# Logits of a soft mixture of experts: four 128-row pieces of g at a time in every second step, in place of two in every step

## The chip, the cores and the metric

The kernel runs on one core of one Trainium2 chip. The metric is the device time of one execution in microseconds, and the time of a kernel is the median of several runs. The engines are called by their names: TensorE (PE in the profile, PEld for its weight loads), VectorE (DVE), ScalarE (ACT), GpSimd (POOL) and SyncE (SP, which only issues DMAs here).

## What is computed

Three stages in float32: attention by chunks of 32 positions with a small context, a feed-forward layer with a rational activation, and a soft mixture of experts.

```python
x = chunk_attention(q, k, v, mem_k, mem_v)     # 3072 tokens x 512
h = x @ w_in                                   # 3072 x 2048
P = a[0] + a[1]*h + a[2]*h**2 + a[3]*h**3
Q = 1.0 + abs(b[0])*abs(h) + abs(b[1])*h**2
g = P / (Q + 1e-6)
x = g @ w_out                                  # 3072 x 512
logits = x @ phi                               # 3072 x 32 slots
d = softmax(logits, axis=0); slot_input = d.T @ x      # 8 experts x 4 slots
slot_out[e] = relu(slot_input[e] @ w1[e]) @ w2[e]      # per expert
out = softmax(logits, axis=1) @ slot_out
```

The kernel never forms `g @ w_out` for all tokens. It uses `wp = w_out @ phi` (2048 x 32), so that logits = g @ wp, and keeps a running sum of d.T @ g, to which w_out is applied once at the end.

## The kernel before

The tokens go in six blocks of 512 (numbered 0 to 5), and the 2048 columns of h in 8 steps of 256 per block. So there are 48 steps k; i = k % 8 is the step's place in its block. One iteration kk of the outer loop (line 569) holds work of several steps, listed in `KN` (line 24) and carried out by `run_step`:

- `h0`, `h1`: the two halves (128 columns each) of h for step kk + 1, 12 float32r matmuls of 128x512 each (`h_part`, line 309). They read x, split in two parts (tiles `xt`), and write one of two PSUM tiles `h`.
- `a1`, `d1`, `a2`, `t`: the rational function of step kk on ScalarE (lines 527, 528, 530, 546, 547) and VectorE (529, 540, 541), a refinement of the reciprocal on POOL (504), and, one iteration later, its end on VectorE (555, 556), which leaves g in a tile `T` (five tiles rotate).
- `p0`, `p1`: `post(k, part)` for step k = kk - 2 (`LATER`: nothing at i = 2, and the steps kk - 3 and kk - 2 at i = 3). Part 0 first does the logits of the step (line 326): two 128x32 pieces of wp as stationary operand against the two 128x512 pieces of g, each piece writing its own strip of 32 rows of one PSUM bank `lg`. The four strips j = 0 to 3 belong to four consecutive pieces of g, so an even step (o = 0) writes strips 0 and 1 and an odd one (o = 1) strips 2 and 3. The strips are summed over the block, and `soft1` adds the four together. Each part then transposes four 128x128 pieces of g into a PSUM bank (line 334), and ScalarE copies them to a tile `g` (line 335). Steps come in pairs that share a `g` tile (`qd`).
- `x1`, `x2`, `x3`: the softmax pieces of the block before. `soft1` (line 341, at i = 1) copies the logits, sums the strips with a matmul (345) and does the running maximum and exponentials (351 to 363); `soft2` (at i = 2) transposes the weights to tokens (370); `soft3` (at i = 2) adds d.T @ g with 16 matmuls of four 32-column pieces each (387), which are four strips side by side as well.
- `at`: one slice of the attention of the block to come (the generator `attention`, line 144). A block has two pairs of 128-token tiles, 18 slices a pair: two of q-k scores (161), six of softmax on VectorE and ScalarE (179 to 188), two of transposes of the weights (196, 198), two of products with v (206), two of normalisation (216), and four of transposes into x and its split (225, 229, 230). Loads of q and k are issued in a pair's third slice, of v in its twelfth. `h0` at i = 7 carries out all slices that are left, for step kk + 1 then belongs to the next block.

Block 0 has a list of its own (`ord0`, with conversions of the weights mixed in), blocks 1 to 4 use `ord`, and the last block, which has no attention to prepare, uses `ordl`. After step 47 iterations 48 and 49 finish the last two steps; the expert part follows, whose weights are loaded into tiles as they come free (`fill`).

The lists give priority. The framework that builds the program keeps data dependences, waits for free tiles, and may put an instruction ahead of one listed earlier that isn't ready yet; so the order of an engine in the trace isn't always the order of the code.

In the profile one float32 matmul of line 326, 345 or 387 is two MATMUL instructions (two passes), one of line 309 or a transpose is one.

Of the kernel before, what the change touches and what calls it, by code (L numbers as in the profile page):

```python
# [19 lines left out]
def float_of_bits(u):  # L20
# [3 lines left out]
KN = {  # L24
    'pre': "q0 i0 v0 q1 o0 v1 i1 o1 s0 A A A A A A A A A A n0 B B B B B B B B B B A A A A A A B B w0 B B B B i2 s1 o2 n1 z0 q2 v2 i3".split(),
    'ord0': "at a1 w1 s2 h0 d1 at t o3 z1 i4 n2 at a2 h1 p0 at p1 at at".split(),
    'ord': "at a1 h0 d1 at t a2 x2 at h1 p0 x1 at p1 x3 at".split(),
    'ordl': "a1 h0 d1 t a2 x2 h1 p0 x1 p1 x3".split(),
}


# [10 lines left out]
def tile_chunk_attention__rational__soft_moe(  # L42
# [15 lines left out]
    PE, ACT, DVE, POOL, SP = nc.tensor, nc.scalar, nc.vector, nc.gpsimd, nc.sync  # L58
# [15 lines left out]
    NF = DFF // P  # L74
# [29 lines left out]
    def bank(shape):  # L104
        return ps_m("m", shape)
# [7 lines left out]
    wp = const("wp", [P, NF, NSLOT])  # L113
# [142 lines left out]
    a0, a1, a2, a3 = (ctab[:, n:n + 1] for n in range(4))  # L256
# [57 lines left out]
    st = {}  # L314

    def post(k, part):

        b, i = divmod(k, NSTEP)
        qd, o = divmod(i, 2)
        t_ = gt_tile[k]  # L320
        if part == 0:
            if i == 0:
                st["lg"] = ps_l("lg", [P, BLK])
            for f2 in range(2):
                j = 2 * o + f2
                PE.matmul(st["lg"][32 * j:32 * j + 32, :], lhsT=wp[:, 2 * i + f2, :], rhs=t_[:, f2, :],  # L326
                          start=(qd == 0), stop=(qd == NF // 4 - 1))
            if o == 0:
                gts[b, qd] = p_g("g", [P, TT, 4 * P])
        pb = bank([P, 2, 2 * P])  # L330
        for m in range(2):
            for f2 in range(2):
                tt = 2 * part + m
                PE.transpose(pb[:, m, f2 * P:f2 * P + P], t_[:, f2, tt * P:tt * P + P], ident)  # L334
        ACT.activation(gts[b, qd][:, 2 * part:2 * part + 2, 2 * P * o:2 * P * o + 2 * P], pb, AF.Copy)  # L335
        if part:
            del gt_tile[k]

    m_run, den, neg_m, alpha = (run[:, n:n + 1] for n in range(4))

# [112 lines left out]
    hs, gt_tile = {}, {}  # L453
# [36 lines left out]
    def w_out_rows(ft):  # L490
        return got["o", ft // 2][:, ft % 2, :]
# [77 lines left out]
    for kk in range(total + 4):  # L569
        b, i = divmod(kk, NSTEP)  # L570
# [31 lines left out]
    for n in range(4):  # L602
        for j in range(4):
            ft = 4 * j + n
            PE.matmul(pb[32 * j:32 * j + 32, :], lhsT=ut[:, n, 32 * j:32 * j + 32],
                      rhs=w_out_rows(ft),
                      start=(n == 0), stop=(n == 3))
# [11 lines left out]
    for eq in range(2):  # L619
        hb = ps_h("h", [P, 2, 512])  # L620
        for c in range(NC):
            for hh in range(2):
                for j in range(4):
                    e = 4 * eq + j
                    PE.matmul(hb[32 * j:32 * j + 32, hh, :], lhsT=sz[:, c, e, :],  # L625
                              rhs=got[("1", e, c)][:, 512 * hh:512 * hh + 512], start=(c == 0), stop=(c == NC - 1))
# [5 lines left out]
        h1 = p_a4("a4", [P, 2, 512])  # L632
# [16 lines left out]
    for eq in range(2):  # L649
        for n in range(8):  # L650
            for j in range(4):
                PE.matmul(so[32 * j:32 * j + 32, :], lhsT=hts[eq][:, n, 32 * j:32 * j + 32],
                          rhs=got[("2", 4 * eq + j, n // 2)][:, n % 2, :],
                          start=(eq == 0 and n == 0), stop=(eq == 1 and n == 7))
# [82 lines left out]
```

## Time and profile before

| | |
|---|---|
| time, median of 3 runs | 634.65 us (632.43 to 635.01) |
| the profiled execution | 633.84 us, span 632.1 us |
| TensorE busy | 561.1 us (89%), weight loads 377.0 us (60%) |
| VectorE busy | 461.8 us (73%) |
| ScalarE busy | 421.4 us (67%) |
| GpSimd busy | 123.5 us (20%) |
| line 309 (h), TensorE | 291.1 us, 1152 instructions |
| line 326 (logits), TensorE | 54.0 us, 192 instructions |
| line 334 (transposes of g), TensorE | 58.2 us, 384 instructions |
| line 387 (soft3), TensorE | 23.5 us, 192 instructions |
| mean granted clock of TensorE | 0.971 of full speed |

The span runs from the first to the last instruction of the profiled execution; the time of that execution includes what lies around it. Busy time of a group is the union of its instructions, so instructions side by side count once; the mean duration of one is another matter, since matmuls are pipelined. The span has four parts: about 64 us of loads and conversions until the first step's activation starts, block 0 with conversions of weights (to 153 us), blocks 1 to 5 (to about 533 us), and a tail with the last softmax, the experts and the output.

### The profile page before, as it was taken

To read this page: it belongs to the slowest core of one execution; us is meant where nothing else is said; L and a number is where in the kernel's file an instruction comes from. 1 tells how busy PE (TensorE), PEld (TensorE's weight loads), DVE (VectorE), ACT (ScalarE), POOL (GpSimd) and SP (SyncE) were. 2 spreads that over 40 slices of the span, in tenths; PEclk is the share of its full clock that TensorE was granted. 3 is DMA by queue.
4 is the path that set the end of the run, shared out by engine and by line. 5 is a ranking of instruction groups with operands and counts; after the bars stand their busy time and mean duration, and the time that the engine had idled before them with its cause. 6 is when DMAs were issued, how large, how long until landed. Compare 5 with 4: busy or idle time off the path is not lost.

```text
span 632.1 us, 13355 instructions
## 1 busy us (share of the span) xinstructions
PE 561.1 (89%) x5784; PEld 377.0 (60%) x5784; DVE 461.8 (73%) x578; ACT 421.4 (67%) x542; POOL 123.5 (20%) x74
## 2 busy tenths in 40 slices
PE   1349999999999999999999999999999997489965
PEld 1338886767666776667765667656776574235211
DVE  3775799977997869978699786997877957620022
ACT  2576899988775878758777586776869688310022
POOL 0121122321231312313133131322223322000000
PEclk9999999999999999999999999999999999689985
DMA  7996745320212202121022210321175236779936
GB/s 308 414 369 218 314 150 200 108 94 1 102 69 90 78 2 101 68 102 67 3 100 68 99 50 21 101 68 63 53 270 184 70 131 226 298 282 409 405 143 266
DMA packets 21754, 97.39 MB, mean 154 GB/s; under 512 B 3136, under 2 KB 3136, under 8 KB 16704
## 3 DMA queue, kind: packets, MB, share of 16 engines
q1 hardware_dynamic: 18000, 79.70, 33.6%
q0 software_dynamic: 2880, 16.78, 7.2%
q8 instruction: 45, 0.74, 0.5%
q10 hardware_dynamic: 816, 0.07, 0.1%
q14 instruction: 13, 0.11, 0.1%
HBM read 86.05 MB, written 10.49 MB: 153 GB/s over the span
## 4 chain that ended last, share of the span: by engine, by line
PE 56%; DVE 18%; ACT 12%; issue 6%; DMA 6%; POOL 1%; DVEq 0%; POOLq 0%; ACTq 0%; SPq 0%
PE h L309 28%; PE lg L326 6%; PE m L334 5%; PE m L387 4%; DMA g<-in_moe_w_in_dram 3%; DVE T L540 3%; DVE T L541 2%; DVE T L555 2%; PE h L625 2%; ACT S L528 2%; ACT g L335 2%; DVE S L529 2%; ACT T L530 2%; DVE T L556 2%; PE h L668 2%
## 5 line engine op out<-in xcount | busy, mean ns | idle before, releaser
L309 PE MATMUL h<-xt,win 128*128 128x512 f32 x1152 | 291.1, 401 | 1.2 <-DVE T L541 0.8
L309 PEld LDWEIGHTS h<-xt,win 128*128 128x128 f32 x1152 | 209.6, 189 | 46.7 <-DVE T L541 1.3
L504 POOL TENSOR_TENSOR S<-S,S 128x1024 f32<-128x1024 f32 x46 | 110.7, 2407 | 315.8 <-DVE S L529 291.0
L529 DVE SCALAR_TENSOR_TENSOR S<-S,S 128x1024 f32<-128x1024 f32 (+1 forms) x49 | 58.8, 1200 | 51.3 <-ACT S L528 51.3
L527 ACT ACTIVATE S<-h,ctab 128x1024 f32<-128x1024 f32 (+1 forms) x49 | 53.7, 1097 | 58.0 <-PE h L309 56.1
L334 PEld LDWEIGHTS m<-ident,T 128*128 128x128 f32 x384 | 42.1, 143 | 46.2 <-issue 22.6
L335 ACT ACTIVATE g<-m 128x512 f32<-128x512 f32 x96 | 55.6, 603 | 18.1 <-PE m L334 18.1
L540 DVE TENSOR_TENSOR T<-T,h 128x1024 f32<-128x1024 f32 (+1 forms) x49 | 58.2, 1188 | 7.6 <-ACT T L530 7.6
L541 DVE SCALAR_TENSOR_TENSOR T<-T,ctab,h 128x1024 f32<-128x1024 f32 (+1 forms) x49 | 61.5, 1254 | 1.3 <-DVE T L540 0.4
L326 PE MATMUL lg<-T,wp 128*32 128x512 f32 x192 | 54.0, 620 | 9.0 <-DVE T L556 9.0
L555 DVE SCALAR_TENSOR_TENSOR T<-T,ctab,S 128x1024 f32<-128x1024 f32 (+1 forms) x49 | 61.3, 1252 | 0.1
L334 PE MATMUL m<-ident,T 128*128 128x128 f32 x384 | 58.2, 285 | 2.3 <-DVE a L182 1.2
L556 DVE SCALAR_TENSOR_TENSOR T<-S,T 128x1024 f32<-128x1024 f32 (+1 forms) x49 | 58.7, 1199 | 1.8
L530 ACT ACTIVATE T<-h,ctab 128x1024 f32<-128x1024 f32 (+1 forms) x49 | 58.9, 1201 | 0.0
L547 ACT ACTIVATE S<-S,ctab 128x1024 f32<-128x1024 f32 (+1 forms) x49 | 55.9, 1144 | 0.6
L546 ACT ACTIVATE S<-S 128x1024 f32<-128x1024 f32 (+1 forms) x49 | 51.5, 1053 | 5.8 <-DVE S L529 3.2
L528 ACT ACTIVATE S<-h,ctab 128x1024 f32<-128x1024 f32 (+1 forms) x49 | 53.7, 1095 | 0.9 <-DVE T L555 0.9
L675 DVE TENSOR_SCALAR xt<-h,csum 128x512 f32<-128x512 f32 x12 | 8.5, 746 | 30.8 <-PE h L668 30.8
L387 PE MATMUL m<-g,ptok 128*32 128x512 f32 x192 | 23.5, 634 | 0.4 <-ACT ptok L372 0.4
L183 ACT ACTIVATE a<-a 128x512 f32<-128x512 f32 x22 | 14.0, 638 | 14.1 <-DVE a L182 14.1
L230 DVE TENSOR_TENSOR xt<-m,xt 128x512 fp32r<-128x512 f32 x24 | 16.5, 688 | 8.5 <-ACT xt L229 8.5
L268 ACT ACTIVATE g<-g 128x1024 uint32<-128x1024 uint32 x16 | 18.5, 1156 | 5.3 <-DMA g<-in_moe_w_in_dram 4.1
(155 smaller groups left out, 614.3 us busy)
## 6 DMA issues: line engine op xcount, KB each, us to landing
win<-in_moe_w_dram SPq DMA_DIRECT2D x32, 512.0 KB, 5.1
k<-in_kw_dram SPq DMA_DIRECT2D x11, 1024.0 KB, 7.4
v<-in_vw_dram SPq DMA_DIRECT2D x11, 1024.0 KB, 4.8
g<-in_moe_w_in_dram POOLq DMA_DIRECT2D x6, 1024.0 KB, 7.3
g<-in_moe_w_out_dram POOLq DMA_DIRECT2D x6, 1024.0 KB, 9.1
out_dram<-xt SPq DMA_DIRECT2D x12, 512.0 KB, 3.2
q<-in_qw_dram SPq DMA_DIRECT2D x11, 512.0 KB, 3.8
T<-in_moe_w_dram SPq DMA_DIRECT2D x10, 512.0 KB, 10.0
```

The lines of the kernel that those rows point to most:

```text
L309: PE.matmul(tile_[:, f2, :], lhsT=ww[:, c, f2 * P:f2 * P + P], rhs=xx[:, c, :], start=(n == 0), stop=(n == 3 * NC - 1))
L326: PE.matmul(st["lg"][32 * j:32 * j + 32, :], lhsT=wp[:, 2 * i + f2, :], rhs=t_[:, f2, :], start=(qd == 0), stop=(qd == NF // 4 - 1))
L334: PE.transpose(pb[:, m, f2 * P:f2 * P + P], t_[:, f2, tt * P:tt * P + P], ident)
L335: ACT.activation(gts[b, qd][:, 2 * part:2 * part + 2, 2 * P * o:2 * P * o + 2 * P], pb, AF.Copy)
L504: (POOL if k < total - 2 else DVE).tensor_tensor(out[:, o], q[:, o], w[:, o], ALU.mult)
L528: ACT.activation(y[:, o], hh[:, o], AF.Square, scale=rb1)
L529: DVE.scalar_tensor_tensor(s[:, o], y[:, o], QC, s[:, o], ALU.add, ALU.add)
L530: ACT.activation(t[:, o], hh[:, o], AF.Identity, bias=a2, scale=a3)
L540: DVE.tensor_tensor(t[:, o], t[:, o], hh[:, o], ALU.mult)
L541: behind[kk] = DVE.scalar_tensor_tensor(t[:, o], t[:, o], a1, hh[:, o], ALU.add, ALU.mult).ins
L555: DVE.scalar_tensor_tensor(t[:, o], t[:, o], a0, w[:, o], ALU.add, ALU.mult)
L556: DVE.scalar_tensor_tensor(t[:, o], e[:, o], 2.0, t[:, o], ALU.subtract, ALU.mult, reverse0=True)
```

## The change

The even step of a pair no longer does its two logits matmuls. The odd step does all four: pieces 0 and 1 from the T tile of the step before, pieces 2 and 3 from its own, in one group of four matmuls, each with its strip of 32 rows. So there are 24 groups of four matmuls where there were 48 of two, with the same 96 matmuls in all. The T tile of an even step is read until then, and both references are dropped after the odd step's second part.

In the lists `ord` and `ordl` the order changes as well. In `ord` the third attention slice, which stood between x2 and h1, and the fourth, which stood behind x1 ahead of p1, are both listed behind p1 and x1 now, one on either side of x3; `soft1` (x1) is listed behind both parts of `post` where it stood between them. `ordl` has this last move alone. `ord0` and `LATER` stay.

```diff
--- before.py
+++ after.py
@@ -24,8 +24,8 @@
 KN = {
     'pre': "q0 i0 v0 q1 o0 v1 i1 o1 s0 A A A A A A A A A A n0 B B B B B B B B B B A A A A A A B B w0 B B B B i2 s1 o2 n1 z0 q2 v2 i3".split(),
     'ord0': "at a1 w1 s2 h0 d1 at t o3 z1 i4 n2 at a2 h1 p0 at p1 at at".split(),
-    'ord': "at a1 h0 d1 at t a2 x2 at h1 p0 x1 at p1 x3 at".split(),
-    'ordl': "a1 h0 d1 t a2 x2 h1 p0 x1 p1 x3".split(),
+    'ord': "at a1 h0 d1 at t a2 x2 h1 p0 p1 x1 at x3 at at".split(),
+    'ordl': "a1 h0 d1 t a2 x2 h1 p0 p1 x1 x3".split(),
 }
 
 
@@ -321,20 +321,21 @@
         if part == 0:
             if i == 0:
                 st["lg"] = ps_l("lg", [P, BLK])
-            for f2 in range(2):
-                j = 2 * o + f2
-                PE.matmul(st["lg"][32 * j:32 * j + 32, :], lhsT=wp[:, 2 * i + f2, :], rhs=t_[:, f2, :],
-                          start=(qd == 0), stop=(qd == NF // 4 - 1))
             if o == 0:
                 gts[b, qd] = p_g("g", [P, TT, 4 * P])
+            else:
+                for j in range(4):
+                    PE.matmul(st["lg"][32 * j:32 * j + 32, :], lhsT=wp[:, 4 * qd + j, :],
+                              rhs=gt_tile[k - 1 + j // 2][:, j % 2, :],
+                              start=(qd == 0), stop=(qd == NF // 4 - 1))
         pb = bank([P, 2, 2 * P])
         for m in range(2):
             for f2 in range(2):
                 tt = 2 * part + m
                 PE.transpose(pb[:, m, f2 * P:f2 * P + P], t_[:, f2, tt * P:tt * P + P], ident)
         ACT.activation(gts[b, qd][:, 2 * part:2 * part + 2, 2 * P * o:2 * P * o + 2 * P], pb, AF.Copy)
-        if part:
-            del gt_tile[k]
+        if part and o:
+            del gt_tile[k - 1], gt_tile[k]
 
     m_run, den, neg_m, alpha = (run[:, n:n + 1] for n in range(4))
```

## Rows read from the trace of the kernel before

**Rows 1.** Windows: length; busy PE, PEld, DVE, ACT, POOL; granted clock, DMA share, GB/s
```profile
100.00:530.00 430.00, 422.39 (x4244) 293.67 (x4244) 362.36 (x414) 328.47 (x416) 107.58 (x48) 1.00 0.25 89
...
320.30:328.34 8.04, 7.69 (x38) 5.28 (x36) 7.96 (x12) 7.21 (x10) 2.42 (x1) 1.00 0.26 110
328.34:341.52 13.18, 12.31 (x180) 8.74 (x177) 13.09 (x19) 9.05 (x14) 2.39 (x1) 1.00 0.24 79
341.52:351.74 10.22, 10.22 (x67) 6.00 (x67) 8.93 (x12) 6.76 (x10) 2.41 (x1) 1.00 0.01 4
...
372.23:382.56 10.33, 10.06 (x170) 7.11 (x168) 9.83 (x11) 7.00 (x9) 2.41 (x1) 1.00 0.31 104
...
sum 79.74, PE 77.99 PEld 53.84 DVE 67.85 ACT 58.65 POOL 19.21; mean PE 9.75 PEld 6.73 DVE 8.48 ACT 7.33 POOL 2.40
```

**Rows 2.** Chain of waits, block 3: start us, duration us, work (x instructions)
```profile
316.05 1.22 DVE T L540
...
338.64 0.69 DVE s L359
...
339.38 0.46 PE m L370 x4
...
342.11 3.57 PE m L387 x32
...
351.64 0.98 PE lg L326 x4
```

**Rows 3.** Timeline: start us, us, engine, line, operation, out<-in, count [idle before <-releaser]
```profile
302.65 1.05 PE L326 MATMUL lg<-T,wp 128*32 128x512 f32 x4
...
303.63 1.09 PE L334 MATMUL m<-ident,T 128*128 128x128 f32 x8
```

**Rows 4.** Timeline, soft3's weight loads at line 387
```profile
342.92 0.13 PEld L387 LDWEIGHTS m<-g,ptok 128*32 128x32 f32 x4 [0.30 <-issue]
343.35 0.13 PEld L387 LDWEIGHTS m<-g,ptok 128*32 128x32 f32 x4 [0.30 <-issue]
```

**Rows 5.** Chain of waits, block 0, last block and tail
```profile
118.52 0.98 PE lg L326 x4
...
478.27 0.98 PE lg L326 x4
...
494.13 0.98 PE lg L326 x2
...
505.24 0.98 PE lg L326 x2
...
529.68 0.98 PE lg L326 x4
...
542.80 1.92 PE lg L326 x4
...
546.62 1.54 PE lg L326 x4
```

**Rows 6.** Timeline of the tail
```profile
543.98 1.29 DVE L556 SCALAR_TENSOR_TENSOR T<-S,T 128x512 f32<-128x512 f32 x2
...
559.07 3.81 SPq L487 DMA_DIRECT2D g<-in_moe_w_dram  x8
```

**Rows 7.** Window ahead of those loads, last columns again DMA share, GB/s
```profile
550.00:560.00 10.00, 6.42 (x41) 1.91 (x39) 4.48 (x14) 2.42 (x7) 0.00 (x0) 0.83 0.39 157
```

**Rows 8.** Timeline at the border of blocks 3 and 4
```profile
385.52 0.62 ACT L229 ACTIVATE xt<-m 128x512 fp32r<-128x512 f32 x1
...
386.17 0.69 DVE L230 TENSOR_TENSOR xt<-m,xt 128x512 fp32r<-128x512 f32 x1 [0.23 <-ACT xt L229]
...
386.66 5.73 PE L309 MATMUL h<-xt,win 128*128 128x512 f32 x24
```

**Rows 9.** Windows, sum of six steps of the last block (iterations 41 to 46)
```profile
sum 50.85, PE 50.85 PEld 34.03 DVE 39.83 ACT 41.12 POOL 14.50; mean PE 8.47 PEld 5.67 DVE 6.64 ACT 6.85 POOL 2.42
```

**Rows 10.** Lines: logits; count | busy us, mean ns | idle before <-releasers
```profile
L326 PE MATMUL lg<-T,wp 128*32 128x512 f32 x192 | 54.0, 620 | 9.0 <-DVE T L556 9.0
```

## The prediction

> **What bounds the kernel now.** I read the windows of the steady stretch first, 100 to 530 us, then those of the steps of one block, then the chain of waits, and last the timeline at the instructions that change.
>
> In these 430 us TensorE is busy for 422.39, VectorE for 362.36 and ScalarE for 328.47, at a granted clock of 1.00 [rows 1]. The steps of block 3 (iterations 24 to 31, i = 0 to 7) tell more. Over the block TensorE is busy 77.99 of 79.74 us and VectorE 67.85, but VectorE is full in i = 1 (7.96 of 8.04) and i = 2 (13.09 of 13.18), while i = 3 is full on TensorE with VectorE at 8.93 of 10.22 [rows 1]. So a block has two parts with different limits: one in which VectorE works without a break, and a longer one in which TensorE does.
>
> The chain of waits says the same. In the first part it runs through VectorE, from line 540 in i = 0 (316.05) to the copy at line 359, whose end releases TensorE's transposes at line 370; from there it is TensorE, with soft3's 32 matmuls and then the logits among the rest [rows 2]. A logits pair stands on that chain with 0.98 us (351.64 is one). Of the eight pairs of a middle block six are on it: two in i = 3 and one each in i = 4, 5, 6 and 7. Those of i = 0 and 1 lie beside VectorE's part.
>
> Is a dense TensorE the bound? The chain says so for the longer part. The Trainium skill, page "Perfetto Trace Analysis", section "Identifying the Most-Contended Engine", calls matmul occupancy a poor measure and would have the weight loads' busy time used. Here that is 293.67 of 430, under VectorE's 362.36 [rows 1], so by that rule VectorE is the engine to relieve. What this would make of the change is an end of the second rival.
>
> **The change, part by part.**
>
> *The matmuls.* A pair is four instructions now (two matmuls, each in two passes). It starts at 302.65 and the transposes behind it at 303.63: 0.98 us [rows 3]. Four pieces side by side aren't shown for logits, but soft3 is the same shape, four 128x32 stationary pieces that write four 32-row strips: its weight loads come four at a time, 0.43 us apart (342.92, 343.35) [rows 4], and its 32 instructions take 3.57 us on the chain [rows 2]. Eight passes of 0.43 leave 0.13 for the ends; a pair is two passes and 0.12. A lone quad is then 2 x 0.43 + 0.13, say 1.00 us. The bounds: 0.89 (3.57 / 4, the ends shared) and 1.96 (four no better than twice two). I take 1.00, for in soft3 the four strips do run in step. TensorE's work falls by 2 x 0.98 - 1.00 = 0.96 for two steps, 23 us for 24 quads.
>
> One rule speaks against a wider group: the Trainium skill, page "TensorE: Matmul & The Clock Gate", section "The cost: per-tile semaphore tail", lets a group end later for each tile that signals. By its figures two tiles more cost 2 x (4.7 + 26.3) = 62 ns a quad, an estimate of 1.5 us over all, and the gain would be smaller by that. The remainders above, 0.13 with four strips and 0.12 with two, don't show it.
>
> *Where the vanished pairs lay.* The pairs of even steps go: in a block those issued in i = 0, 4 and 6 and one of the two in i = 3.
> - Blocks 1 to 4: three each on the chain (i = 3, 4, 6), 12 x 0.98 = 11.8. The pair of i = 0 lies beside VectorE's part, and TensorE waits at line 370 anyway: I count nothing for it. If it paid, 0.98 in each of four blocks.
> - Block 0: one of the first two and the one at 118.52 [rows 5], 2.0. The third lies beside ScalarE's work: nothing, or 0.98.
> - Last block: three, the first at 478.27 and the last at 529.68, 2.9; and the pair of step 40, which is torn into halves of 0.98 each at 494.13 and 505.24 [rows 5], 2.0.
>
> Together 18.7. The quads that stay on the chain (three in each of blocks 1 to 4, one in block 0, three in the last) are longer by 0.02: 16 x 0.02 = 0.3.
>
> *The tail.* Behind the last h matmuls VectorE sets the pace; then a pair of 1.92 us at 542.80, eight transposes, and a pair of 1.54 us at 546.62 stand in a row [rows 5]. The first pair goes, but the quad has to wait for the last step's g, which VectorE ends at 543.98 + 1.29 = 545.27 [rows 6]: 546.62 - 545.27 = 1.35 gained. Against it, soft1 is now listed behind the second group of transposes. Eight take 546.62 - 542.80 - 1.92 = 1.90 here, so four 0.95, of which I take a good half, 0.55 (bounds 0 and 0.95), since ScalarE's copy of the logits runs beside them. Net 0.8. The weight loads into the g tiles, issued at 559.07 [rows 6], move with it: the DMA engines are at 0.39 just before [rows 7], so nothing is late there that was on time.
>
> *The reordering.* In the middle blocks the third attention slice moves from ahead of h1 to behind both groups of transposes, and the fourth from between these to behind soft1. VectorE's order of work stays, except that soft1 stands ahead of a slice; POOL's queue (line 504) isn't passed. The loads of q and k in a third slice move too, but their tiles are free only when the second q-k slice is done, and that one stays; nothing else is queued on SP behind them in these blocks. On TensorE five slices a block move: one of q-k scores, two of transposed weights, one of products with v, and one of the last x transposes. The last matters: h0 of the next block can't start before x is split. Now the second x copy starts at 385.52, its split (line 230) ends at 386.86, and h starts at 386.66 without a wait [rows 8]. With both groups of x transposes behind h1, their two copies come one behind the other on ScalarE, so I count x ready one copy later, 0.62 [rows 8], at four borders: 2.4. Bounds: 0, as now, and 3.8 a border (behind twelve h matmuls, half of 5.73 [rows 8], and eight transposes, 1.0 [rows 3], with no cover).
>
> *Buffers.* An even step's T tile is kept until the odd step's quad, three iterations behind its own instead of two. Five tiles rotate, so it is needed in the fifth: more than an iteration to spare, and I count nothing. Were that cover gone, ScalarE's line 530 would wait for the quad, and all of VectorE's polynomial behind it.
>
> Sum: 18.7 - 0.3 + 0.8 - 2.4 = 16.8. The profiled execution took 633.84 us, 632.1 of it the span, and lies 0.8 below the median of the runs shown, 634.65. Forecast: 633.84 - 16.8 = 617.0 us.
>
> **The rivals.**
>
> *Everything pays.* The five pairs off the chain count too (4.9) and the borders stay free (2.4): 617.0 - 7.3 = 609.7. For it: VectorE has gaps in every block (67.85 of 79.74). Against it: the wait on line 359 [rows 2].
>
> *VectorE and ScalarE take over.* In i = 6 VectorE is busy 9.83 of 10.33 [rows 1], so that not even 0.98 fits there, and ScalarE has 41.12 of 50.85 in six steps of the last block [rows 9]. If i = 6 gives nothing and i = 3 half of its 0.98, a middle block gains 1.5; with three fifths of the 6.9 of block 0 and the last block, 4.1, the sum is 4 x 1.5 + 4.1 - 0.3 = 9.8: 624.0. With VectorE as the bound throughout nothing is gained, 634: this is where the rule on weight loads leads. Against that end stand VectorE's gaps.
>
> *The quads are torn.* The order on an engine isn't always that of the code: a logits group gives way where other work comes ready in its middle, as in the halves at 494.13 and 505.24. Each tear costs 0.98, and with 24 the gain is gone: 634. Against it: of the 192 / 4 = 48 pairs [rows 10] two were torn, and soft3's 32 stay together.
>
> *Slower: attention comes late at the border.* Two of the moved slices of a block's second pair (transposed weights, x) can each be 3.8 us later. If one lateness adds to the other, 7.6; less a cover of 2.0 (a quad, eight transposes) TensorE waits 5.6 at each of five borders, 28 us: 633.84 - 19.2 + 28 = 642.6, where 19.2 is the sum without the border. It makes the kernel slower from a lateness of 19.2 / 5 + 2.0 = 5.8 us on. Against it: the slices move within their iteration only, and x is ready in time now with h of the old block still ahead of it.
>
> **How the numbers follow.** Forecast (612 to 622): 0.50. Everything pays (below 612): 0.12. Others take over (622 to 630): 0.18. No change (torn quads, VectorE throughout): 0.10. Slower: 0.10. Half a per cent, 3.2 us, is about what a measurement of this kernel can tell from no change. So faster 0.80, same 0.10, slower 0.10. The range goes from 609, where everything pays, to 627, beyond the second rival's 624 and with the borders' dearer cost partly in it (two of four at 3.8); about 0.2 is left out.
>
> **What would show it.** Right: line 326 in 24 groups of eight instructions with some 1.00 us to the next, and its busy time near 24 us instead of 54.0 [rows 10]; i = 3, 4 and 6 shorter by about 1 us, i = 1 and 2 as now; TensorE's wait at line 370 longer by up to 1 us. Wrong: line 326 in smaller groups, or a quad above 1.5 us; VectorE full in i = 3 to 6; TensorE at i = 7 waiting more than 2 us for line 229 or 230.

## The result, and the profile after

The changed kernel takes 614.63 us (median of 4 runs, 614.39 to 615.33) against 634.64 for the kernel before on the same chip: a ratio of 0.970, 95% interval 0.968 to 0.972. The forecast was 617.0, in a range of 609 to 627. The profiled execution took 614.68 us, 612.9 of them the span; before it was 633.84 and 632.1. So the two spans differ by 19.2 us where the sum had 16.8.

Where the time went is read from four stretches that follow one another: block 0, blocks 1 to 4, the last block, and the tail. The windows of before (columns as in [rows 1]):

```profile
64.52:152.94 88.42, 86.64 (x907) 66.84 (x905) 75.73 (x86) 78.55 (x100) 21.49 (x15) 1.00 0.41 151
152.94:472.93 319.99, 313.27 (x3496) 216.80 (x3495) 273.31 (x322) 235.62 (x302) 76.79 (x32) 1.00 0.22 77
472.93:533.49 60.56, 60.05 (x298) 39.59 (x297) 46.41 (x46) 49.48 (x60) 16.91 (x7) 1.00 0.42 141
533.49:632.07 98.58, 70.16 (x437) 28.16 (x434) 27.11 (x53) 22.88 (x41) 0.95 (x1) 0.81 0.77 302
```

The same windows of the changed kernel:

```profile
65.04:154.91 89.87, 86.35 (x908) 66.77 (x906) 75.64 (x86) 78.95 (x100) 22.40 (x15) 1.00 0.41 148
154.91:458.90 303.99, 298.19 (x3496) 215.96 (x3495) 263.36 (x322) 235.63 (x301) 77.03 (x32) 1.00 0.23 81
458.90:515.10 56.20, 54.59 (x293) 39.25 (x293) 45.76 (x47) 48.43 (x60) 16.85 (x7) 1.00 0.41 148
515.10:612.90 97.80, 70.26 (x441) 28.73 (x437) 27.13 (x53) 22.83 (x41) 0.95 (x1) 0.81 0.79 308
```

| stretch | forecast | measured |
|---|---|---|
| loads until the first step | 0 | +0.5 |
| block 0 | -2.0 | +1.5 |
| blocks 1 to 4 | -11.8 + 0.2 + 2.4 = -9.2 | -16.0 |
| last block | -4.9 + 0.1 = -4.8 | -4.4 |
| tail | -0.8 | -0.8 |
| span | -16.8 | -19.2 |

In blocks 1 to 4 TensorE's busy time falls by 15.1 us (313.27 to 298.19), and the time by 16.0: what TensorE no longer does is all gained there, at the same granted clock of 1.00. The tail's difference is no firm reading. In kernels that do the same work there, its length goes with its granted clock: in the runs below 95.67 us at 0.84 and 100.26 at 0.78.

The groups by line, logits (columns as in [rows 10]):

```profile
L328 PE MATMUL lg<-T,wp 128*32 128x512 f32 x192 | 34.8, 618 | 0.8 <-DVE T L557 0.8
```

The busy time fell from 54.0 us [rows 10] to 34.8, not to the forecast's 24. The chain of waits says why. A lone quad is as forecast, 1.00 us in all places of this kernel where it stands whole at a granted clock of 1.00; this is one, and the next is the place at i = 7 of block 2, the border to block 3 (columns as in [rows 2]):

```profile
286.67 1.00 PE lg L328 x8
...
297.88 0.97 PE lg L328 x2
298.85 0.59 PE m L225 x4
299.44 0.99 PE lg L328 x6
300.43 1.02 PE m L335 x8
301.45 5.55 PE h L309 x24
```

This quad is torn: one matmul (two passes), four transposes of x, then the other three matmuls. The first piece takes 0.97 alone and the second 0.99, so the tear costs a whole 0.97 of TensorE's time. All four blocks 1 to 4 show it, and both later quads of block 0 are torn too, one of them into three pieces. With 7 pieces too many, 7 x 0.97 = 6.8 us of TensorE's time go that way. One more quad, in the last block, is halved by a wait for VectorE and not by other matmuls, and the one in the tail takes 1.94 us, at a lower granted clock. The chain also shows that h stands right behind, at 301.45, without the wait for x that the forecast priced at 2.4.

Last, the windows of steps i = 1 to 6 of block 3, and the block's sum:

```profile
314.64:322.36 7.72, 7.17 (x40) 4.97 (x37) 7.66 (x12) 7.35 (x10) 2.41 (x1) 1.00 0.30 128
322.36:334.84 12.48, 11.65 (x180) 8.51 (x177) 12.17 (x20) 9.05 (x15) 2.40 (x1) 1.00 0.25 87
334.84:345.06 10.22, 10.22 (x68) 6.25 (x67) 9.22 (x12) 6.88 (x10) 2.40 (x1) 1.00 0.00 0
345.06:355.77 10.71, 10.70 (x182) 8.13 (x180) 6.67 (x8) 7.82 (x11) 2.39 (x1) 1.00 0.40 148
355.77:362.80 7.03, 6.76 (x36) 5.04 (x38) 6.64 (x12) 7.03 (x11) 2.41 (x1) 1.00 0.01 3
362.80:372.60 9.80, 9.80 (x175) 7.66 (x168) 9.32 (x10) 7.04 (x10) 2.41 (x1) 1.00 0.31 109
...
sum 75.88, PE 74.22 PEld 53.52 DVE 65.66 ACT 58.72 POOL 19.25; mean PE 9.28 PEld 6.69 DVE 8.21 ACT 7.34 POOL 2.41
```

The steps i = 4 and 5 of before, beside those of [rows 1]:

```profile
351.74:363.86 12.12, 11.85 (x178) 7.90 (x176) 8.40 (x11) 7.89 (x11) 2.38 (x1) 1.00 0.37 130
363.86:372.23 8.37, 8.37 (x46) 6.23 (x44) 7.03 (x10) 7.66 (x10) 2.39 (x1) 1.00 0.01 4
```

The block is 3.86 us shorter, but only in part in the steps forecast. Of i = 3, 4 and 6, i = 3 stays at 10.22, i = 4 loses 1.4 and i = 6 0.5. Of the others, which should not have moved, i = 5 loses 1.3, i = 1 and 2 lose 0.3 and 0.7, and i = 7, with the torn quad, takes 0.4 more. Step 2 is no longer full on VectorE (12.17 of 12.48).

### The profile page after: what moved, and what is told of

It reads as the page before. It is cut to its first block, busy times and chain, and to the rows that moved or that the text cites. A ratio compares the mean times of both kernels' runs of the same rounds, so it can differ in the third digit from the quotient of the medians.

```text
span 612.9 us, 13366 instructions
## 1 busy us (share of the span) xinstructions
PE 540.5 (88%) x5784; PEld 376.4 (61%) x5784; DVE 451.4 (74%) x578; ACT 420.7 (69%) x542; POOL 124.6 (20%) x74
## 3 DMA queue, kind: packets, MB, share of 16 engines
q1 hardware_dynamic: 18000, 79.70, 34.8%
## 4 chain that ended last, share of the span: by engine, by line
PE 60%; DVE 14%; ACT 11%; issue 6%; DMA 6%; POOL 2%; POOLq 0%; DVEq 0%; ACTq 0%; SPq 0%
PE h L309 30%; PE m L335 6%; PE lg L328 4%; PE m L388 4%; DMA g<-in_moe_w_in_dram 3%; ACT S L528 3%; ACT S L529 2%; PE m L161 2%; PE h L626 2%; PE m L414 2%; POOL S L505 2%; DVE T L542 2%; DVE T L541 2%; PE h L669 2%; PE m L225 2%
## 5 line engine op out<-in xcount | busy, mean ns | idle before, releaser
L335 PEld LDWEIGHTS m<-ident,T 128*128 128x128 f32 x384 | 44.0, 143 | 33.3 <-issue 22.8
L335 PE MATMUL m<-ident,T 128*128 128x128 f32 x384 | 53.4, 279 | 8.9 <-DVE T L557 7.7
L336 ACT ACTIVATE g<-m 128x512 f32<-128x512 f32 x96 | 53.6, 604 | 9.6 <-PE m L335 8.4
L328 PE MATMUL lg<-T,wp 128*32 128x512 f32 x192 | 34.8, 618 | 0.8 <-DVE T L557 0.8
```

The source lines that it names most:

```text
L328: PE.matmul(st["lg"][32 * j:32 * j + 32, :], lhsT=wp[:, 4 * qd + j, :], rhs=gt_tile[k - 1 + j // 2][:, j % 2, :], start=(qd == 0), stop=(q ...
```

## The experiments

The theory: TensorE's time for the logits is paid except in VectorE's part, and the new lists cost a little. The rivals: the lists themselves give something; the mere move of the logits pays; a new wait takes part of the gain.

**Each part alone.** First the merged quads with the old lists:

```diff
-    'ord': "at a1 h0 d1 at t a2 x2 h1 p0 p1 x1 at x3 at at".split(),
-    'ordl': "a1 h0 d1 t a2 x2 h1 p0 p1 x1 x3".split(),
+    'ord': "at a1 h0 d1 at t a2 x2 at h1 p0 x1 at p1 x3 at".split(),
+    'ordl': "a1 h0 d1 t a2 x2 h1 p0 x1 p1 x3".split(),
```

> The four-strip groups of the change with the lists of before. Theory (the four strips side by side take work from TensorE, and a pair that vanishes from its part of a block pays 0.98 us): nearly the whole gain is here, 612 to 617 us against 614.6 for the change and 634.6 before; line 328 busy 25 to 35 us. Rival (the new order of the attention slices brings a good part of the gain, for the middle blocks gained 3.7 to 4.5 us each where 2.35 was forecast): 622 us or more.

Then the new lists with the old pairs: the function `post` as before, `ord` and `ordl` as after.

```diff
+            for f2 in range(2):
+                j = 2 * o + f2
+                PE.matmul(st["lg"][32 * j:32 * j + 32, :], lhsT=wp[:, 2 * i + f2, :], rhs=t_[:, f2, :],
...
-            else:
-                for j in range(4):
...
```

> The new lists with the pairs of before, one pair in every step. Theory: the order alone gains nothing, 633 to 638 us (the 2.4 us for x at the borders may show as a loss). Rival (the order itself gains): 622 to 629 us.

Measured: the quads alone 620.62 us, ratio 0.978 (0.974 to 0.982); the lists alone 628.65, ratio 0.991 (0.988 to 0.994). Both are faster by more than the noise, the lists alone by less than 1%: 13.9 and 5.9 us by the medians, together 19.7, near the 20.0 of the change. The first lies between its two expectations, the second is where the rival had it. The windows of blocks 1 to 4, quads alone and then lists alone:

```profile
154.29:461.89 307.60, 297.73 (x3492) 216.70 (x3491) 261.03 (x321) 234.26 (x299) 76.95 (x32) 1.00 0.23 80
```

```profile
151.80:466.83 315.03, 309.09 (x3495) 215.84 (x3493) 272.36 (x322) 237.76 (x301) 76.71 (x32) 1.00 0.22 78
```

The quads alone gain 12.4 us here (319.99 to 307.60), where the forecast's terms for them come to 11.8 - 0.2 = 11.6. The same window for the logits' line alone, before and then quads alone (length; busy PE, PEld; clock, DMA share, GB/s):

```profile
152.94:472.93 319.99, 34.09 (x130) 4.61 (x128) 1.00 0.22 77
```

```profile
154.29:461.89 307.60, 17.07 (x130) 2.52 (x128) 1.00 0.23 80
```

Here no quad is torn, and the logits take half of what they took. Of the 17.0 us saved, 12.4 are gained; TensorE's idle time, length less busy, grows from 6.7 to 9.9, and the q-k scores take 1.4 us more (14.97 to 16.34 by their line's window). The sum's 11.6 would put that down to the pairs of i = 0, with a longer wait behind line 359 (360 now). But the waits of TensorE in these blocks (engine, tile and line, releaser: us in all, times, longest) tell another thing:

```profile
PE m L335 <- ACT g L336: 6.1, 12, 0.7
...
PE m L371 <- DVE s L360: 0.3, 1, 0.3
```

The wait of the sum went down, to 0.3 us from 2.6 before. In its place the transposes of g wait 12 times for a PSUM bank that ScalarE's copy (line 336) has still to empty, twice at the turn from i = 3 to 4 and once some 18 us later, in each of the four blocks. Line 102 gives these tiles three banks in all, and the slices of attention draw on them too. The reading: with a pair of 0.98 us less between two groups of transposes, TensorE is back for a bank sooner than ScalarE, with its own 1.1 to 1.2 us instructions ahead of the copy, sets one free. Before there are 4 such waits, 1.1 us in all (an expectation below calls them absent), and in the change none.

The lists alone gain 5.0 us, where the forecast counted a loss of 2.4. TensorE's busy time falls by 4.2, though it does the same work, and its idle time by 0.8. Where that is shows in the timeline, at the turn from i = 3 to 4 of block 3 (columns as in [rows 3]), before:

```profile
354.12 0.66 PE L334 MATMUL m<-ident,T 128*128 128x128 f32 x4
354.71 1.02 PE L161 MATMUL m<-k,q 64*32 64x64 f32 x66
355.65 0.66 PE L334 MATMUL m<-ident,T 128*128 128x128 f32 x4
356.24 0.54 PE L161 MATMUL m<-k,q 64*32 64x64 f32 x34
357.05 0.66 PE L334 MATMUL m<-ident,T 128*128 128x128 f32 x4 [0.27 <-ACT g L335]
357.63 0.44 PE L161 MATMUL m<-k,q 64*32 64x64 f32 x28
```

and with the lists alone:

```profile
351.10 1.09 PE L334 MATMUL m<-ident,T 128*128 128x128 f32 x8
...
352.49 0.60 PE L334 MATMUL m<-ident,T 128*128 128x128 f32 x4
353.02 1.53 PE L161 MATMUL m<-k,q 64*32 64x64 f32 x128
```

In the old order a slice of q-k scores stands between the two groups of transposes, and its 128 matmuls are cut into 66, 34 and 28 by transposes that come ready in between. In the new order it runs in one piece. Four transposes between other shapes take 0.59 us (355.65 to 356.24), eight in a row not 1.18 but 1.02 by the chain; the three pieces of the slice take 0.94, 0.54 and 0.37 (the chain has the last), 1.85 together, the whole one 1.46. Over blocks 1 to 4 the groups of eight transposes at this line number 14 before and 21 with the lists alone. The lines' windows agree: q-k scores 14.97 to 13.32, products with v 14.82 to 13.53, transposes of g 39.96 to 38.21. The three fall by 4.7 together, while the line of h rises by 1.7 (193.11 to 194.76); busy times of lines overlap a little, so these are no sum.

The Trainium skill, "TensorEngine Tiling (Array Packing)", section "Key Properties", says that a change of the tiling mode drains the engine, and gives no price. The shapes that alternate here (128x128, 64x64 and 128x32) differ in that way, and the 0.59 against a half of 1.02 bears the direction out; that draining is the cause wasn't tried by itself.

**Which part of the lists.** The quads with the old lists once more, but in blocks 1 to 4 the fourth slice moved from between the groups of transposes to the end; the third stays ahead of h1, and `soft1` between the parts of `post`:

```diff
-    'ord': "at a1 h0 d1 at t a2 x2 at h1 p0 x1 at p1 x3 at".split(),
+    'ord': "at a1 h0 d1 at t a2 x2 at h1 p0 x1 p1 x3 at at".split(),
```

> The quads with the lists of before, but in blocks 1 to 4 the fourth attention slice moved from between the two groups of transposes to the end of the iteration; the third slice stays where it was. With the quads and the lists of before, line 335 waits 12 times in blocks 1 to 4 for ScalarE's copy at line 336 to free one of the three PSUM banks, 6.1 us in all, in i = 3 and i = 5; before and in the change these waits are absent. Theory: the fourth slice, which takes banks between the two groups, makes them. Then they are gone here (below 1 us in all), blocks 1 to 4 take 304 to 305.5 us, and the whole 615.5 to 618. Rival: the third slice, which stands ahead of h1, makes them, or both do; then 8 to 12 of the waits stay, blocks 1 to 4 take 306.5 to 308, and the whole 619 to 621.

And the change with `soft1` alone put back between the two parts, both slices as after:

```diff
-    'ord': "at a1 h0 d1 at t a2 x2 h1 p0 p1 x1 at x3 at at".split(),
+    'ord': "at a1 h0 d1 at t a2 x2 h1 p0 x1 p1 at x3 at at".split(),
```

> As the change, but in blocks 1 to 4 soft1 stands between the two groups of transposes again, as before; the two attention slices stay behind them. Theory (the order gains by keeping matmuls of one shape together, mostly transposes of g and the slices): blocks 1 to 4 within 1 us of the change's 304.0 us together, the whole 614 to 616 us. Rival (it is the earlier soft1 that relieves VectorE's stretch): 306 or more, the whole 617 or more.

Measured: 616.39 us, ratio 0.974 (0.969 to 0.979), and 615.6, ratio 0.972 (0.970 to 0.975). Blocks 1 to 4 of the two:

```profile
154.59:460.07 305.48, 296.48 (x3492) 216.98 (x3491) 262.93 (x321) 235.03 (x300) 77.11 (x32) 1.00 0.23 81
```

```profile
152.95:457.57 304.62, 298.33 (x3496) 216.99 (x3495) 263.81 (x322) 234.89 (x302) 77.13 (x32) 1.00 0.23 81
```

With the fourth slice moved, all 12 waits for the copy are gone, so it was the slice that took the banks. Of their 6.1 us, 2.1 are gained (307.60 to 305.48), 1.3 of them in TensorE's busy time, for another wait comes in: the last x transposes for the normalisation, whose place in the order is now later,

```profile
PE m L225 <- DVE a L216: 3.3, 4, 0.8
```

With the third slice moved too, that wait is gone, but the quad of i = 7 is torn (12 whole quads in these blocks in place of 16). The place of `soft1` gives 0.6 us at most (304.62 against 303.99), as much as kernels with the same lists in these blocks differ by (303.99, 304.10 and 304.69 in three of them, one execution each).

**Moved, not merged.** The logits of both steps in the odd step, but two strips ahead of each group of transposes:

```diff
-            else:
-                for j in range(4):
-                    PE.matmul(st["lg"][32 * j:32 * j + 32, :], lhsT=wp[:, 4 * qd + j, :],
-                              rhs=gt_tile[k - 1 + j // 2][:, j % 2, :],
...
+        if o:
+            for j in range(2 * part, 2 * part + 2):
+                PE.matmul(st["lg"][32 * j:32 * j + 32, :], lhsT=wp[:, 4 * qd + j, :],
+                          rhs=gt_tile[k - 1 + part][:, j % 2, :],
...
```

> As the change, but the odd step does its four matmuls as two pairs, one ahead of each group of transposes, so never four strips side by side. Theory: 48 groups of 0.98 us are back, TensorE's work is that of before, 631 to 638 us. Rival (moving the logits out of the even steps is what frees the engines, the strips don't matter): 614 to 620 us.

Measured: 632.2 us, ratio 0.997 (0.995 to 0.999); blocks 1 to 4:

```profile
156.84:474.29 317.45, 312.95 (x3494) 217.03 (x3491) 263.38 (x322) 236.78 (x302) 76.99 (x32) 1.00 0.22 78
```

That is 13.5 us more than after, with the same lists and the same matmuls in the same steps; TensorE is busy 14.8 us longer. So four strips side by side are what pays, not that the even step is rid of its logits. This run tells one thing more. VectorE's busy time is as low as in the change (263.38, where before had 273.31), TensorE's is about that of before (312.95 against 313.27), and the blocks are only 2.5 us shorter than before. Relief of VectorE without relief of TensorE gave no more than that.

**Pairs put back in one place.** With the new lists, the pairs of i = 0 and 1 (steps 6 and 7 of a block, blocks 1 to 4), those of i = 4 and 5 (steps 2 and 3), or those of block 0 were put back into their own steps:

```diff
-            else:
+            if qd == 3 and b < 4:
+                for j in range(2 * o, 2 * o + 2):
+                    PE.matmul(st["lg"][32 * j:32 * j + 32, :], lhsT=wp[:, 4 * qd + j, :], rhs=t_[:, j % 2, :],
+                              start=(qd == 0), stop=(qd == NF // 4 - 1))
+            elif o:
```

> As the change, but the last quad of each of blocks 0 to 3 is two pairs again, in their own steps, so that four pairs come back at i = 0 and four quads at i = 1 become pairs, all beside VectorE's stretch. TensorE's work rises by 4 x 0.96 = 3.8 us. Theory (in that stretch VectorE sets the pace and TensorE waits at the transposes of soft2 for it): the time rises by at most 1 us, 614 to 616 us, and that wait shrinks. Rival (TensorE sets the pace there too): 618 to 619 us.

With the condition `qd == 1 and 0 < b < 5`:

> The same at another place: in blocks 1 to 4 the second quad is two pairs again, issued in i = 4 and 5, in TensorE's stretch. The same 3.8 us of work. Theory: it is paid in full, 618 to 619 us. Rival (VectorE's stretch decides a block, TensorE catches up elsewhere): 614 to 616 us.

With `b == 0`:

> Quads in blocks 1 to 5, pairs in block 0, where the change took 89.9 us against 88.4 before instead of the 2.0 us less that were forecast. In its trace three extra pieces of torn quads and a wait of 1.5 us for a PSUM bank stand there. Theory (the loss comes from the new order that the quads bring about among the conversions of the weights): block 0 takes 88 to 89 us again and the time is 612 to 614 us. Rival (the loss is a difference between executions): 614.6 or more.

Measured: 615.95 us, ratio 0.973 (0.970 to 0.975); 617.28, ratio 0.974 (0.969 to 0.979); 613.55, ratio 0.969 (0.966 to 0.972). Blocks 1 to 4 of the first, the same of the second, and block 0 of the third:

```profile
153.48:460.36 306.88, 301.81 (x3496) 216.07 (x3495) 268.05 (x322) 236.17 (x301) 77.06 (x32) 1.00 0.23 80
```

```profile
154.72:460.58 305.86, 300.69 (x3496) 215.90 (x3495) 268.13 (x322) 235.95 (x302) 76.97 (x32) 1.00 0.23 81
```

```profile
64.53:153.00 88.47, 86.67 (x907) 66.84 (x906) 75.66 (x86) 78.58 (x101) 21.51 (x15) 1.00 0.41 150
```

Four more pairs are 3.9 us of logits. At i = 0 and 1 they cost 2.9 us of time, where nothing was forecast; at i = 4 and 5 1.9, where the whole 3.9 was. TensorE's busy time rises by 3.6 and 2.5 us, so about four fifths and three quarters of what TensorE does in addition is paid. The difference between the two is near the spread of 0.7 seen above, but neither fits its forecast: under the new lists both places pay, in part. The whole times alone wouldn't show it: the first fits its theory, and the runs of the second go from 613.38 to 619.44.

In block 0 of this change the pairs are the better choice: 88.47 us, as before (88.42), against 89.87 with quads. TensorE is busy as long in both (86.67 and 86.35), so the quads cost idle time there: with them, transposes of the weights at line 406 wait 1.5 us for a bank that the copy at line 336 empties, and line 414 waits 1.1 for ScalarE in place of 0.4. The first of these waits begins on VectorE, as the chain of waits of the change shows (columns as in [rows 2]):

```profile
123.80 3.03 DVE win L271
126.85 0.61 ACT g L336
127.50 1.15 PE m L406 x8
```

Line 271, part of the conversion of the weights, takes 1.22 us elsewhere and 3.03 here, where it starts beside a refinement on GpSimd (123.02 to 125.74); the copy waits for it, and TensorE for the copy. With pairs line 271 doesn't meet the refinement. What comes of block 0 in the whole, 1.1 us by the medians, the intervals can't tell apart.

**The tear at i = 7.** In the new order the x transposes, carried out with all slices left at i = 7, come ready in the middle of the quad. This edit puts the quad ahead of them, and leaves i = 6 one slice for later:

```diff
-        for what in KN["ord0" if b == 0 else "ord" if b < NBLK - 1 else "ordl"]:
+        order = KN["ord0" if b == 0 else "ord" if b < NBLK - 1 else "ordl"]
+        if 0 < b < NBLK - 1 and i == 6:
+            order = order[:-1]
+        if 0 < b < NBLK - 1 and i == 7:
+            order = ["p0", "at"] + [w for w in order if w != "p0"]
+        for what in order:
```

> As the change, but at i = 7 of blocks 1 to 4 the logits and the first transposes are listed ahead of the last x transposes, which move from the end of i = 6 to behind them. In the trace of the change these four quads are torn (two instructions, four x transposes, six instructions), which costs 0.97 us each. Theory: the groups are whole and 3.9 us come back: 610 to 612 us. Rival (x decides when the next block's h can start, so that the time goes into a wait for x): 614 to 616 us.

Measured: 619.37 us, ratio 0.978 (0.974 to 0.982), slower than both expectations. The tears are gone from these blocks (22 quads of 24 are whole, in place of 18), and the logits there are 2.4 us shorter (21.24 to 18.81 by the line's window); not 3.9, for each of the four quads takes 1.43 us here. But now a slice of q-k scores at the border is cut, into 20, 2 and 42 matmuls, and that line takes 1.9 us more (14.59 to 16.53). TensorE is busy as long as in the change (298.26 against 298.19), so the edit took no work from it, and yet the blocks take 308.10, 4.1 more than after, all of it idle time of TensorE. It waits longer behind line 360 for VectorE, 5.6 us in place of 2.3 in these blocks. The timeline at i = 2 of block 3:

```profile
329.34 2.38 POOL L505 TENSOR_TENSOR S<-S,S 128x1024 f32<-128x1024 f32 x1 [6.74 <-DVE S L530]
...
329.83 1.90 DVE L353 TENSOR_TENSOR bm<-bm,run 128x1 f32<-128x1 f32 x1
...
336.21 0.46 PE L371 MATMUL m<-ident,s 64*128 64x64 f32 x4 [2.40 <-DVE s L360]
```

and of the change itself:

```profile
328.23 0.15 DVE L353 TENSOR_TENSOR bm<-bm,run 128x1 f32<-128x1 f32 x1
...
328.46 2.40 POOL L505 TENSOR_TENSOR S<-S,S 128x1024 f32<-128x1024 f32 x1 [6.67 <-DVE bm L353]
...
332.92 0.46 PE L371 MATMUL m<-ident,s 64*128 64x64 f32 x4 [0.81 <-DVE s L360]
```

The running maximum at line 353, one column, takes 0.15 us when it starts ahead of GpSimd's refinement and 1.90 when it starts beside it: it ends 0.01 us after GpSimd does (331.73, 331.72). What follows on VectorE up to line 360 is late by that, and TensorE waits 2.40 in place of 0.81. The same happens in block 2 (1.92 us). So most of the loss is a new wait, which falls in VectorE's part.

**The wait of VectorE for GpSimd.** Such waits are in every kernel here. Before, line 187 (1e-9 added to 128x8 sums) shows them:

```profile
208.95 1.57 DVE L187 TENSOR_SCALAR sm<-sm 128x8 f32<-128x8 f32 x1
```

It started inside a refinement on GpSimd that ran from 208.10 to 210.49, and ended at 210.52. Of its 24 cases the 10 that started beside GpSimd took 1.57 us in the median and the other 14 0.17. Four reductions (line 186), the one reciprocal and the operations with one operand in PSUM that started beside GpSimd were not lengthened. The Trainium skill, "SBUF — State Buffer", section "Who interferes with whom", has a port that VectorE shares with GpSimd, needed by VectorE's faster copies and scalar operations and by operations with two operands in SBUF, and never by a reduction; the trace agrees: line 293, with two operands in SBUF, took 2.33 and 2.55 us beside GpSimd and 1.22 elsewhere, as line 271 did above. Line 555, with two as well, was never lengthened, but its ten cases beside GpSimd all started in the last 0.2 us of the GpSimd operation, so they show nothing.

So a first kernel wrote both small operations, lines 187 and 353, as another instruction:

```diff
-            DVE.tensor_scalar(sm, sm, 1e-9, None, ALU.add)
+            DVE.scalar_tensor_tensor(sm, sm, 1e-9, sm, ALU.add, ALU.max)
-            DVE.tensor_tensor(bm, bm, m_run, ALU.max)
+            DVE.scalar_tensor_tensor(bm, bm, 1.0, m_run, ALU.mult, ALU.max)
```

> As the change, but two small VectorE operations are written in another form with the same result: the addition of 1e-9 at line 187 and the running maximum at line 353 as scalar_tensor_tensor. In the trace of before line 187 takes 165 ns, but 1572 ns where a GpSimd operation runs beside it, and the maximum 160 and 878; the scalar_tensor_tensor of line 555 takes 1280 beside GpSimd as without. Theory (VectorE sets the pace in i = 0 to 2, and these waits are part of its work): the wait of TensorE at the transposes of soft2 goes down, and the four middle blocks gain 0.5 to 1.5 us each: 609 to 613 us. Rival (the waits lie beside other waits, or the new form waits as well): 614 to 615.5 us.

Measured: 614.89 us, ratio 0.970 (0.966 to 0.974), and blocks 1 to 4 took 304.10: nothing changed. The new instruction waited as well:

```profile
208.44 0.95 DVE L187 SCALAR_TENSOR_TENSOR sm<-sm 128x8 f32<-128x8 f32 x1
```

The GpSimd operation that runs here ends at 209.36, and this one at 209.39; away from GpSimd it takes 0.16 in the median. The expectation was built on line 555's cases, which show nothing; in this form too the operation, now with two operands in SBUF, waits.

The next kernel has the whole quad at i = 7 (the edit above) and does without both operations. The 1e-9 is left out: it is added to a sum that is at least 1, where float32 doesn't hold it. The maximum is a reduction over two columns, the second of which holds the running maximum:

```diff
-            DVE.tensor_scalar(sm, sm, 1e-9, None, ALU.add)
...
+    both_m = const("both_m", [P, 2])
+    m_run = both_m[:, 1:2]
...
-            DVE.tensor_reduce(bm, lt, AX.X, ALU.max)
-            DVE.tensor_tensor(bm, bm, m_run, ALU.max)
+            DVE.tensor_reduce(both_m[:, 0:1], lt, AX.X, ALU.max)
+            DVE.tensor_reduce(bm, both_m, AX.X, ALU.max)
```

> As e4_i7_whole (whole groups at i = 7), with the two small VectorE operations that wait for GpSimd gone: the running maximum at line 353 is a reduction over two columns, and the addition of 1e-9 at line 187 is left out (the sum is at least 1, float32 doesn't feel it). In e4 line 353 took 1.9 us in blocks 2 and 3, up to the end of a GpSimd operation, and TensorE waited 2.4 us for what follows it, against 0.15 and 0.8 in the change. Theory (this wait ate the work that the whole groups save): blocks 1 to 4 take 300 to 304 us together (e4 308.1, the change 304.0), the whole 609 to 615 us, by the clock in the tail. Rival (the loss of e4 has another place, as x at the border): blocks 1 to 4 stay at 307 to 309.

And these two edits alone on the change, without the edit of i = 7, but with the pairs in block 0:

> As the change, with pairs in block 0 (as e7_pairs_block0) and without the two waits for GpSimd (as e9). Theory: VectorE's stretch is shorter by up to 0.9 us in each of blocks 1 to 4 (line 187 takes 0.8 to 0.95 in one of two cases there): blocks 1 to 4 at 301 to 304 us together, block 0 at 88 to 89, the whole 609 to 613 us. Rival (VectorE's waits lie beside others, TensorE sets the pace): 304 or more together, the whole 613 to 615.

Measured: 610.26 us, ratio 0.963 (0.960 to 0.967), and 612.69, ratio 0.970 (0.965 to 0.974). Blocks 1 to 4 of the first and of the second:

```profile
152.01:453.72 301.71, 298.12 (x3496) 217.09 (x3495) 256.57 (x306) 234.41 (x302) 77.02 (x32) 1.00 0.23 82
```

```profile
155.93:459.23 303.30, 298.72 (x3496) 215.72 (x3495) 257.54 (x306) 235.51 (x301) 77.06 (x32) 1.00 0.23 81
```

VectorE works some 6 us less than in the change, 263.36 to 256.57 and 257.54. With the change's order that gives 0.7 us of time (303.99 to 303.30), no more than the spread. With the whole quad it gives 6.4 (308.10 to 301.71), and turns the loss of 4.1 into a gain of 2.3. So the waits for GpSimd made the loss. The gain isn't the price of the tears: TensorE is busy as long as in the change (298.12 against 298.19), and what falls is its idle time, from 5.8 to 3.6 us. The 0.97 us of a tear are TensorE's work; what mending one gives in time these runs don't show.

A good part of this version's advantage lies in block 0, with the quads in it:

```profile
65.08:152.01 86.93, 84.48 (x908) 66.70 (x907) 72.25 (x81) 78.48 (x100) 21.96 (x15) 1.00 0.41 151
```

That is 2.9 us less than after and 1.5 less than before. Line 271 isn't lengthened here, the wait for the bank is gone, and one of the two torn quads is whole. The second kernel's block 0, with pairs, took 90.44 us where 88 to 89 was expected, but at a granted clock of 0.98, so the two can't be compared. The first version is the fastest: its interval ends at 0.967 and the change's own begins at 0.968.

## Why the prediction was right, and where it wasn't

The forecast was 2.4 us too high, and its main step holds: TensorE is the bound in most of a block, and a vanished pair there is worth its 0.98 us. Not all of its terms hold; two of them failed in opposite directions.

- *The matmuls.* Right: the quad takes 1.00 us, the bounds were 0.89 and 1.96, and with two strips at a time the change gives almost nothing. The estimate of 62 ns a quad beside it isn't borne out: 1.00 against 0.98 for a pair.
- *Where the vanished pairs lay.* Right in size for the last block, 4.4 against 4.8, and with the old lists for blocks 1 to 4, 12.4 against 11.6; but there for another reason than the one given: what isn't paid went into waits for banks and into q-k scores that are cut up more, not into VectorE's part, and the wait behind line 359 didn't grow. Its split by step was wrong in part: i = 3 gave nothing, and i = 5 gave 1.3 us. Pairs put back at i = 0 and 1 cost 2.9 us and not nothing, at i = 4 and 5 1.9 and not 3.9. The step took the chain of before for a property of the stages; the change moves TensorE's work between them, and a step that was full on VectorE no longer is.
- *Block 0.* Failed: 2.0 forecast, 1.5 lost. Both later quads are torn, and TensorE waits 1.5 us for a bank, behind a copy that itself waits for line 271, which met a refinement on GpSimd; with pairs in block 0 these waits are gone, and so is the loss. In the version without lines 187 and 353 block 0 is 1.5 us shorter than before with its quads, so most of the 2.0 may lie there once these waits are away; no run with pairs, without those operations and at the same clock stands beside it. The prediction had no rival for banks, nor for a VectorE operation that comes to lie beside GpSimd: the wait for banks is in the trace of before with 1.1 us in blocks 1 to 4, and the step didn't ask what it becomes when TensorE arrives earlier.
- *The reordering.* Failed in sign: a cost of 2.4 was forecast for x at the borders, of which the change shows no wait and the lists alone four of 0.3 us at most, 1.0 together; against it a gain of 5.0 with the lists alone. The step looked only for who waits, and asked nothing of what TensorE's own instructions cost in another order, nor which banks the moved slices leave free for the quads' neighbours. Pieces of one shape left together are shorter than the same pieces cut up, and the rows for it were there: 0.98 for each half of a torn pair [rows 5].
- *The tail.* 0.8 forecast, 0.8 measured at a granted clock of 0.81 in both; since the clock alone moves this stretch by more, it is not shown.
- *Buffers.* Right: ScalarE has no idle time ahead of line 531, which writes the T tiles (0.0 in the groups by line).
- *The rivals.* "The quads are torn" was a quarter right: 6 of 24, 6.8 us of TensorE's time, which is most of why the logits' line stands at 34.8 and not 24. "Everything pays" was nearer than its chance said: the borders are free. VectorE as the bound throughout is refuted: with quads alone TensorE's work was cut, VectorE has the same instructions, and 13.9 us came of it. VectorE's busy time fell too, though, since line 187 waited less for GpSimd (14.5 us in blocks 1 to 4 before, 5.0 with quads alone, 7.6 after); taking the rest of that wait away gave 0.7, and with the logits moved but not merged VectorE's relief gave 2.5 at most. Attention late at the border didn't occur; that rival counts five borders where slices move at four, so its 28 us should have been 22.4, its 642.6 about 637, and the lateness from which it makes the kernel slower 6.8 us and not 5.8.

The total came out well in part by luck: block 0 (3.5 us worse than forecast) and blocks 1 to 4 (6.8 us better) stand against each other. The second is about what the lists give, 5.0 in place of -2.4, less what the four tears take of it.

Open stays how the shares add up to the last microsecond: the two parts alone come to 12.4 + 5.0 = 17.4 us in blocks 1 to 4, and the change has 16.0. It has none of the waits for the copy, which the quads alone have, and four tears, which neither part has alone; no run has the one without the other at the change's own order. The one edit that made the quads at i = 7 whole cut a slice of q-k scores instead. Nor was the kernel before run without line 187: what its shorter waits give in i = 1 and 2, which are 1.0 us shorter together in block 3, is not measured; the run with the logits moved but not merged, where TensorE's busy time is as before, lets no more than 2.5 us for the four blocks be expected of it.

## What to carry to other kernels

When small matmuls of different shapes share TensorE, cost the order as well as the count: look in the timeline for groups that are cut into pieces, before and after, and price each piece from the rows. When a group is made larger, look for what may come ready in its middle, for the piece that is left costs as much as a whole group; and when a tear is mended, look whether TensorE's busy time fell, for the cut may have moved to another group. When work is taken from the bounding engine, ask what it now reaches sooner (here a bank that another engine still had to empty), and trace each new wait back to the first operation that became longer.

## What the runs showed of the hardware

Float32 matmuls with 32 columns of stationary operand that write four different strips of 32 rows take 1.00 us for four in the change (1.43 at i = 7 where the quad stands ahead of the x transposes), 0.98 for two, and 0.97 for one alone (297.88 above). A VectorE operation on a 128x1 column, 0.15 us, took 1.90 where it started beside a GpSimd operation on 128x1024 elements, and one on 128x1024 elements with two operands in SBUF 3.03 in place of 1.22 (line 271). Reductions were the way around it, while a scalar-tensor-tensor operation with both operands in SBUF was not.
